# Turning the probabilities in two half-height array tiles, with the short pieces in spare PSUM columns

## The chip, the cores and the metric

The kernel runs on one core of a Trainium2 chip. The metric is the device time of one execution in microseconds (us), taken on that core. Below, PE is TensorE's matmul stream and PEld its weight loads, DVE is VectorE, ACT is ScalarE, POOL is GpSimd and SP is the queue that issues nearly all DMAs.

## The reference

Attention with a bias made from positions, and behind it a two-layer block. What is computed, cut to its core:

```python
scores = (1/sqrt(64)) * q @ k.T                 # 4 batches, 8 heads, 576 positions, 64 wide
x = log1p(|i - j|) / log1p(max(i, 1))           # for each query i and key j
scores += relu(x * w1 + b1) @ w2                # one bias matrix of 576 x 576 for each head
attn = exp(scores - max); attn /= attn.sum(-1) + 1e-9
y = attn @ v                                    # heads side by side: 2304 rows of 512
h = relu(y @ w_in)                              # 512 -> 2048
out = (s * h * h + b) @ w_out                   # 2048 -> 512
```

## The kernel before

It has three stages. Up to about 60 us it builds the bias matrices and writes them to DRAM. Then comes the attention stage, to about 345 us. From there on PE runs the two-layer block nearly without a pause.

The attention stage works on 16 pairs (one head, two batches x = 0 and 1). A pair has five units: units t = 0 to 3 hold 128 query rows of both batches, unit t = 4 holds the last 64 rows of both batches in one 128-row tile. A unit n goes through these operations, in this order:

- `scores(n)`: PE multiplies queries and keys (three float32r products each) into one PSUM tile `sps` of two banks for each x. The 64-row contractions of x = 0 and x = 1 stand in the two halves of the array's rows. The pool `ps_s` has two such tiles, so the next unit's scores need the tiles that this unit's scores left.
- `biased(n, x)` (L242): DVE adds the bias, and takes the row minimum `mn`.
- `expo(n, x)` (L253): ACT takes the exponential into `pr` and sums the row into `su`.
- `probs_t(n, part)`: PE turns `pr` through transposes into PSUM tiles `tps` (pool `ps_t`, two banks), and ACT or DVE copies them to `pt` (512 of the keys) and `ptr` (the last 64 keys of each batch; the "short" transpose).
- `norm(p)` takes the reciprocal of the pair's sums, `norm_t` turns them on PE and copies them to `rt`, `norm_store` and `norm_load` take them through DRAM to `rb`.
- `av(p, kb, hf)`: PE multiplies the values with `pt` or `ptr` into `xps`. At a pair's end DVE multiplies `xps` by `rb` (L340) and a DMA writes the result to `xt` in DRAM.

The order of every engine's queue is the order in which the code is written (a manual schedule). A call `step(n)` with u = n mod 5 issues, for three different units at once, the scores of unit n + 2, the turning of unit n, the exponentials of unit n + 2, and a fifth of the output product of the pair before:

```python
        if ok(m, 0):
            scores(m)
            biased(m, 0)
        if ok(m, 1):
            biased(m, 1)
```

Behind these each step calls `fill()` once or twice (twice for even u). Each call issues one fifth of the decoding of one weight block for the block that follows: first an ACT conversion (L372), then a POOL operation (L374), then three DVE operations (L376, L379, L382). So a pair has eight such calls: in the mean 1.6 conversions on ACT and 4.8 operations on DVE. `split_qk` on POOL (L203, L204) splits the next pair's queries and keys into two float32r parts. At the end of the stage `load_x` and `split_x` (L418) fetch the block's first input from `xt`.

Of the kernel before, what the change touches and what calls it, by code (L numbers as in the profile page):

```python
# [9 lines left out]
F32 = mybir.dt.float32  # L10
# [3 lines left out]
AF = mybir.ActivationFunctionType  # L14
# [12 lines left out]
def attention_moe(ctx, tc, q, k, v, w_in, w_out, dist, par, out):  # L27
    nc = tc.nc
    NB, H, S, D = 2 * q.shape[0], q.shape[1], k.shape[3] - 64, q.shape[2] // 2
# [4 lines left out]
    HALF = S // 2  # L34
# [7 lines left out]
    LAST = 5 * NP  # L42
# [10 lines left out]
    ps_t = ps_ctx.enter_context(tc.tile_pool(name="ps_t", bufs=2, space=PSUM))  # L53
# [13 lines left out]
    ident = const.tile([128, 128], F32, name="ident")  # L67
# [97 lines left out]
    qs, ks, vals, tts, bts, pts, units, accs = {}, {}, {}, {}, {}, {}, {}, {}  # L165
    sums, rows, rts, rbs, bes = {}, {}, {}, {}, {}
# [47 lines left out]
    def scores(n):  # L214
        p, t = divmod(n, 5)
        qt, kt = qs[p], ks[p]
        c = slice(128 * t, 128 * t + 128)
        xs = range(width(n))
        ps = [ps_s.tile([128, 2, 512], F32, tag="s", name="sps") for _ in xs]
        mms = []  # L220
        for hf in range(2):
            for x in xs:
                d = slice(64 * x, 64 * x + 64) if t < 4 else slice(0, 128)
                o = hf * HALF + (64 if x == 0 else 0)
                for i, (a, b) in enumerate(((0, 0), (0, 1), (1, 0))):
                    mms.append((i, hf, x, ps[x][:, hf, 0:HALF], qt[d, a, c], kt[d, b, o:o + HALF]))
        for i, _, _, o, a, b in sorted(mms, key=lambda e: e[1::-1]):
            nc.tensor.matmul(o, a, b, start=(i == 0), stop=(i == 2))  # L228
        units[n] = (
            tp.tile([128, 2, S], F32, tag="pr", name="pr"),  # L230
            sm.tile([128, 2], F32, tag="mn", name="mn"),
            ps,
        )
        if t == 0:
            sums[p] = sm.tile([128, 9], F32, tag="su", name="su")

    def biased(n, x):
# [25 lines left out]
    def norm(p):  # L263
        su = sums.pop(p)
        nc.vector.tensor_scalar(su, su, 1e-9, None, op0=ALU.add)
        nc.vector.reciprocal(su, su)
        rows[p] = su

    def norm_t(p, ps):
        nc.tensor.transpose(ps[0:9, 128:256], rows.pop(p), ident)  # L270
        rt = sm.tile([9, 128], F32, tag="rt", name="rt", bufs=2)
        nc.vector.tensor_copy(rt, ps[0:9, 128:256])
        rts[p] = rt

    def norm_store(p):
# [6 lines left out]
    def norm_load(p):  # L282
        rbs[p] = tp.tile([128, S], F32, tag="rb", name="rb", bufs=2)
        for x in range(2):
            nc.sync.dma_start(out=rbs[p][64 * x:64 * x + 64, :], in_=rs_d[p][x:x + 1, :].broadcast_to([D, S]))

    def probs_t(n, part):
        p, t = divmod(n, 5)
        pr = units[n][0]
        if p not in pts:  # L290
            pts[p] = (ptp.tile([128, 4, 2, S], F32, tag="pt", name="pt"),
                      ptp.tile([128, S], F32, tag="ptr", name="ptr"))
        pt, ptr = pts[p]
        ps = ps_t.tile([128, 512], F32, tag="t", name="tps")
        c = slice(128 * t, 128 * t + 128)
        if t < 4 and part < 2:
            for kb in range(4):
                nc.tensor.transpose(  # L298
                    ps[:, 128 * kb:128 * kb + 128],
                    pr[:, part, 64 * part + 128 * kb:64 * part + 128 * kb + 128], ident)  # L300
            o, i = pt[:, :, part, c], ps.rearrange("p (a b) -> p a b", a=4)
            if part == 0:
                nc.scalar.activation(o, i, AF.Copy)
            else:
                nc.vector.tensor_copy(o, i)
        elif t < 4:
            nc.tensor.transpose(ps[:, 0:128], pr.rearrange("p x j -> p (x j)")[:, 512:640], ident)  # L307
            nc.scalar.activation(ptr[:, c], ps[:, 0:128], AF.Copy)  # L308
        elif part == 0:
            for kb in range(4):  # L310
                nc.tensor.transpose(  # L311
                    ps[:, 128 * kb:128 * kb + 128], pr[:, 0, 128 * kb:128 * kb + 128], ident)
            nc.vector.tensor_copy(
                pt[:, :, :, 512:S], ps.rearrange("p (a x b) -> p a x b", a=4, x=2))
        else:
            nc.tensor.transpose(ps[0:64, 0:128], pr[:, 0, 512:S], ident)  # L316
            for x in range(2):
                nc.scalar.activation(  # L318
                    ptr[64 * x:64 * x + 64, 512:S], ps[0:64, 64 * x:64 * x + 64], AF.Copy)
            norm_t(p, ps)  # L320

    def av(p, kb, hf):
        h, b0 = pairs[p]
        pt, ptr = pts[p]
        vt = vals[p]
        if kb == 0 and hf == 0:
            accs[p] = ps_x.tile([128, 2, 512], F32, tag="x", name="xps")
        ps = accs[p]
        c = slice(hf * HALF, (hf + 1) * HALF)
        if kb < 4:  # L330
            for x in range(2):
                nc.tensor.matmul(ps[64 * x:64 * x + 64, hf, 0:HALF], vt[:, 4 * x + kb, :], pt[:, kb, x, c],  # L332
                                 start=(kb == 0), stop=False)
# [133 lines left out]
    def ok(n, x):  # L467
        return 0 <= n < LAST and x < width(n)
# [7 lines left out]
    def step(n):  # L476
        p, u = divmod(n, 5)
        m = n + 2
        cur = 0 <= n < LAST
        if ok(m, 0):  # L480
            scores(m)
            biased(m, 0)
        if ok(m, 1):
            biased(m, 1)
        if cur and u == 3:
            norm(p)
        if cur:
# [43 lines left out]
    def fill():  # L531
        next(filler, None)
# [16 lines left out]
        26: ((load_bias, 0, 2, 3),),  # L549
        33: ((scores, 0), (biased, 0, 0), (expo, 0, 0), (biased, 0, 1)),  # L550
        35: ((expo, 0, 1), (scores, 1), (biased, 1, 0),
             (expo, 1, 0), (biased, 1, 1), (expo, 1, 1), (load_w, *early[0]), (load_w, *early[1]),
             (load_q, 2), (load_k, 2), (load_v, 1)),
    }
    for st in range(STEPS):
# [74 lines left out]
    for i in range(2, len(todo) + LAG):  # L630
        if i < len(todo):
            c, f = todo[i]
            if c == 0 and f in (6, 10):
# [3 lines left out]
                    name=f"w3{kind}", bufs=1, side=("left", "right")[kind], reuse_waits="tile"))  # L637
# [84 lines left out]
```

## Time and profile before

| | |
|---|---|
| median of 3 runs | 746.71 us (746.08 to 747.33) |
| span of the profiled execution (its own time; the page has no other) | 747.1 us |
| PE busy over the span | 716.6 us (96%) |
| DVE, ACT, POOL busy | 429.3 us (57%), 363.5 us (49%), 186.3 us (25%) |
| attention stage, 180 to 325 us (145 us) | PE busy 140.56 us, DVE 122.98 us, ACT 101.30 us, POOL 45.93 us |

Busy shares of the whole span mix the stages: from 347 us on DVE and ACT have little to do, so what they do in the attention stage has to be read from stretches of that stage alone. A step of the attention stage takes 3.40 us, a pair 16.87 us where nothing is waited for.

### The profile page before, as it was taken

Reading aid. Unit: us, or ns where it says so; the run is one execution under the profiler, and the core shown is the slowest. Engines: PE = TensorE matmul, PEld = TensorE weight load, DVE = VectorE, ACT = ScalarE, POOL = GpSimd, SP = SyncE. Lnnn points to the kernel's source line nnn. Section 1 sums busy time; section 2 is a strip of 40 time slices with the busy share of each in tenths; the row PEclk is TensorE's granted clock in tenths of the full one; section 3 lists DMA queues with packets and bytes.
Section 4 is the critical chain, followed back from the end, with each engine's and each line's share of the span. In section 5 each row is a group of like instructions: output and inputs, shape, how many; then the busy total and the mean of one; then the engine's idle time right before and its main releaser. Section 6 shows DMA issues by size and latency. Waiting matters only on the chain.

```text
span 747.1 us, 12023 instructions
## 1 busy us (share of the span) xinstructions
PE 716.6 (96%) x4530; PEld 534.9 (72%) x4530; DVE 429.3 (57%) x794; ACT 363.5 (49%) x756; POOL 186.3 (25%) x194
## 2 busy tenths in 40 slices
PE   8978999899999999969999999999999999999998
PEld 4436666666666666646888888888888888888896
DVE  7976888788888878963288632233332332223332
ACT  7967767576666667653445322232222332222332
POOL 7991534445333234203654100000000000000000
PEclk9999999999999999989999999999999999999999
DMA  5977765556564765351012130000300002000100
GB/s 171 297 205 245 227 204 170 176 156 212 160 215 134 228 214 184 97 176 60 13 57 85 29 114 0 1 1 0 113 1 0 1 1 84 1 0 1 57 1 28
DMA packets 39817, 76.98 MB, mean 103 GB/s; under 512 B 9040, under 2 KB 12368, under 8 KB 39760
## 3 DMA queue, kind: packets, MB, share of 16 engines
q1 hardware_dynamic: 39616, 75.90, 32.4%
q8 instruction: 35, 0.57, 0.3%
q10 hardware_dynamic: 144, 0.33, 0.1%
q14 instruction: 22, 0.18, 0.1%
HBM read 55.45 MB, written 20.13 MB: 101 GB/s over the span
## 4 chain that ended last, share of the span: by engine, by line
PE 81%; issue 3%; POOL 3%; ACT 2%; DVE 1%; DMA 1%; SPq 1%; DVEq 0%; ACTq 0%; POOLq 0%
PE hps L429 27%; PE o L453 27%; PE sps L228 8%; PE xps L332 7%; PE tps L298 7%; PE xps L335 2%; PE tps L307 2%; PE tps L311 1%; POOL kr L204 1%; ACT ptr L318 1%; DMA x<-xt 1%; POOL qr L204 1%; PE tps L270 1%; POOL full L374 0%; PE tps L316 0%
## 5 line engine op out<-in xcount | busy, mean ns | idle before, releaser
L453 PE MATMUL o<-who,gt 128*128 128x512 f32 x576 | 192.5, 393 | 0.0
L429 PE MATMUL hps<-x,whi 128*128 128x512 f32 (+1 forms) x640 | 184.5, 373 | 0.0
L434 DVE SCALAR_TENSOR_TENSOR r<-r,sb 128x512 f32<-128x512 f32 (+1 forms) x80 | 56.7, 708 | 193.2 <-ACT r L433 193.2
L433 ACT ACTIVATE r<-hps 128x512 f32<-128x512 f32 (+1 forms) x80 | 44.4, 555 | 227.5 <-PE hps L429 227.5
L429 PEld LDWEIGHTS hps<-x,whi 128*128 128x128 f32 x640 | 117.5, 189 | 24.1 <-issue 0.4
L453 PEld LDWEIGHTS o<-who,gt 128*128 128x128 f32 x576 | 108.3, 188 | 24.1
L429 PE MATMUL hps<-x,wli 128*128 128x512 f32 (+1 forms) x320 | 119.0, 372 | 0.0
L253 ACT ACTIVATE pr<-tt,mn 128x576 f32<-128x576 f32 x144 | 110.1, 767 | 10.3 <-DVE mn L242 9.7
L453 PE MATMUL o<-wlo,gt 128*128 128x512 f32 x288 | 113.2, 393 | 0.0
L242 DVE CUSTOM_DVE_ANT_0 tt<-sps,bt 128x576 f32<-128x576 f32 x128 | 91.6, 753 | 29.4 <-PE sps L228 24.0
L228 PEld LDWEIGHTS sps<-kr,qr 64*128 64x128 f32 (+1 forms) x864 | 67.8, 185 | 39.6 <-issue 10.1
L228 PE MATMUL sps<-kr,qr 64*128 64x288 f32 (+1 forms) x864 | 88.3, 311 | 5.8 <-POOL kr L204 2.7
L439 DVE SCALAR_TENSOR_TENSOR gt<-r,sb,gt 128x512 fp32r<-128x512 f32 (+1 forms) x80 | 56.3, 704 | 54.0 <-ACT gt L438 54.0
L438 ACT ACTIVATE gt<-r,sb 128x512 fp32r<-128x512 f32 (+1 forms) x80 | 54.4, 680 | 52.2 <-DVE r L434 52.2
L298 PE MATMUL tps<-ident,pr 128*128 128x128 f32 x512 | 77.1, 282 | 0.3 <-ACT ptr L308 0.3
L332 PE MATMUL xps<-pt,vt 128*64 128x288 f32 x512 | 76.5, 421 | 0.0
L429 PEld LDWEIGHTS hps<-x,wli 128*128 128x128 f32 x320 | 60.3, 188 | 11.1
L298 PEld LDWEIGHTS tps<-ident,pr 128*128 128x128 f32 x512 | 57.7, 142 | 11.4 <-ACT ptr L308 11.2
L453 PEld LDWEIGHTS o<-wlo,gt 128*128 128x128 f32 x288 | 54.2, 188 | 11.6
L374 POOL TENSOR_SCALAR full<-full 128x512 f32<-128x512 f32 x32 | 22.6, 705 | 115.1 <-ACT full L372 114.6
L332 PEld LDWEIGHTS xps<-pt,vt 128*64 128x64 f32 x512 | 31.5, 137 | 24.3 <-issue 10.6
L136 PE MATMUL bps<-f,pt__110 128*32 128x512 f32 x288 | 42.8, 599 | 5.3 <-POOL f L119 2.2
(69 smaller groups left out, 748.1 us busy)
## 6 DMA issues: line engine op xcount, KB each, us to landing
bias<-stg SPq DMA_DIRECT2D x36, 288.0 KB
raw<-in_moe_w_in_dram SPq DMA_DIRECT2D x16, 512.0 KB
raw<-in_moe_w_out_dram SPq DMA_DIRECT2D x16, 512.0 KB
bt<-bias SPq DMA_DIRECT2D x7, 1152.0 KB
qt<-in_q_dram SPq DMA_DIRECT2D x16, 320.0 KB
kt<-in_k_dram SPq DMA_DIRECT2D x16, 320.0 KB
vt<-in_v_dram SPq DMA_DIRECT2D x16, 320.0 KB
rb<-rs SPq DMA_DIRECT2D x32, 144.0 KB
```

Of the source, the lines that this page charges most:

```text
L136: nc.tensor.matmul(pb[32 * c:32 * c + 32, 0:512], w2bd, fs[c][0][:, 0:8], start=True, stop=True)
L228: nc.tensor.matmul(o, a, b, start=(i == 0), stop=(i == 2))
L242: nc.vector.tensor_tensor_reduce(tt.rearrange("p (a b) -> p a b", a=2), ps[x][:, :, 0:HALF], bias.rearrange("p (a b) -> p a b", a=2), -1.0 ...
L253: nc.scalar.activation(pr[:, x], tts.pop((n, x)), AF.Exp, bias=mn[:, x:x + 1], scale=-1.0, accum_out=sums[p][:, col:col + 1])
L298: nc.tensor.transpose(ps[:, 128 * kb:128 * kb + 128], pr[:, part, 64 * part + 128 * kb:64 * part + 128 * kb + 128], ident)
L332: nc.tensor.matmul(ps[64 * x:64 * x + 64, hf, 0:HALF], vt[:, 4 * x + kb, :], pt[:, kb, x, c], start=(kb == 0), stop=False)
L429: nc.tensor.matmul(ps[:, 0:n], w[0, g][:, a, fc], xs_t[c, a][:, j, 0:n], start=(i == 0), stop=(i == 3 * KB - 1))
L433: nc.scalar.activation(r, ps[:, 0:n], AF.Relu)
L434: nc.vector.scalar_tensor_tensor(r, r, sb[:, 0:1], r, op0=ALU.mult, op1=ALU.mult)
L438: nc.scalar.activation(hi, r, AF.Identity, bias=sb[:, 1:2])
L439: nc.vector.scalar_tensor_tensor(lo, r, sb[:, 1:2], hi.bitcast(F32), op0=ALU.add, op1=ALU.subtract)
L453: nc.tensor.matmul(os_t[c][i], gt[:, a, tok], w[1, g][:, fo], start=(f == 0 and j == 0), stop=(f == NF - 1 and j == 2))
```

## The change

The transposes of a unit's probabilities become twice as many of half the size. Rows 0 to 63 and rows 64 to 127 of `pr` are turned separately, in the two halves of the array's rows, alternately, each half into a PSUM bank of its own (the two `ps_t` tiles). The short transpose no longer has a `ps_t` tile: it is written to columns 288 and up of the score tile of the next unit (`spare(n)`), which the scores leave free; the pair's sums go there too. For u = 2 (where the scores that follow use all 128 rows) and for the last two units the transposes keep the full height. The step has a new order: transposes, scores, output product. The exponential of x = 1 leaves the end of its own step and is issued in the next one, behind the copy of the short transpose (`later`).

```diff
+    def spare(n):
+        if n + 1 < LAST - 1:
+            return units[n + 1][2][0][:, :, HALF:]
+        return ps_t.tile([128, 512], F32, tag="t", name="tps").rearrange("p (a b) -> p a b", a=2)
...
+        pss = [ps_t.tile([128, 512], F32, tag="t", name="tps") for _ in range(2)]
+        su = rows.pop(p) if t == 4 else None
+        for i in range(-2, 8):
+            for r in range(2):
+                d = slice(64 * r, 64 * r + 64)
+                if t < 4 and i >= 0:
+                    kb, x = divmod(i, 2)
+                    k0 = 64 * x + 128 * kb
+                    o, b = pss[r][:, 64 * i:64 * i + 64], pr[d, x, k0:k0 + 128]
+                elif t < 4:
+                    if i == -1:
+                        continue
+                    o, b = end[:, r, 0:64], pr[d].rearrange("p x j -> p (x j)")[:, 512:640]
...
+                nc.tensor.transpose(o, b, ident[d, d])
+        if t < 4:
+            nc.scalar.activation(
+                ptr[:, c].rearrange("p (a b) -> p a b", a=2), end[:, :, 0:64], AF.Copy)
...
+        later(n + 1)
+        if t == 4:
+            norm_copy(p, end[0:9, :, 64:128])
...
+            if r == 0:
                 nc.scalar.activation(o, i, AF.Copy)
             else:
                 nc.vector.tensor_copy(o, i)
...
+    def later(n):
+        if (n, 1) in tts:
+            expo(n, 1)
...
+        if cur:
+            probs_t(n)
         if ok(m, 0):
             scores(m)
             biased(m, 0)
...
-        if cur:
-            for part in (2, 0, 1) if u < 4 else (1, 0):
-                probs_t(n, part)
         if ok(m, 0):
             expo(m, 0)
-        if ok(m, 1):
-            expo(m, 1)
         if p >= 1:
             av(p - 1, u, 0)
```

On PE, the steps u = 3 and u = 4 of a pair stood like this before (L228 scores, L307 and L316 short transpose, L298 and L311 the others, L270 the sums, L332 and L335 output product):

```order
L228 MATMUL sps<-kr,qr 128x288 x12
L307 MATMUL tps<-ident,pr 128x128
L298 MATMUL tps<-ident,pr 128x128 x8
L332 MATMUL xps<-pt,vt 64x288 x4
L228 MATMUL sps<-kr,qr 128x288 x12
L316 MATMUL tps<-ident,pr 64x128
L270 MATMUL tps<-ident,su 9x128
L311 MATMUL tps<-ident,pr 128x128 x4
L335 MATMUL xps<-ptr,vt 128x288 x2
```

And now, the same two steps on PE (all half-height transposes are L352):

```order
L352 MATMUL sps<-ident,pr 128x64 x2
L352 MATMUL tps<-ident,pr 128x64 x16
L228 MATMUL sps<-kr,qr 128x288 x12
L387 MATMUL xps<-pt,vt 64x288 x4
L352 MATMUL sps<-ident,pr 64x64 x2
L352 MATMUL sps<-ident,su 9x64 x2
L352 MATMUL tps<-ident,pr 128x64 x8
L228 MATMUL sps<-kr,qr 128x288 x12
L390 MATMUL xps<-ptr,vt 128x288 x2
```

The transposes moved from behind the scores to ahead of them, and the short ones and the sums now write `sps`, the tile of the next unit's scores.

On ACT, the steps u = 3, u = 4 and the start of the next u = 0 stood like this before (L308 and L318 copies of the short transpose, L303 copy to `pt`, L253 exponentials, L372 a conversion of the decoding):

```order
L308 ACTIVATE ptr<-tps 128x128
L303 ACTIVATE pt<-tps 128x4x128
L253 ACTIVATE pr,su<-tt,mn 128x576 x2
L372 ACTIVATE full_986<-raw 128x512
L318 ACTIVATE ptr<-tps 64x64 x2
L253 ACTIVATE pr,su<-tt,mn 128x576 x2
L308 ACTIVATE ptr<-tps 128x128
L303 ACTIVATE pt<-tps 128x4x128
```

And now, the same place on ACT (L354 and L358 copy the short transpose, L369 copies to `pt`, L427 is the conversion):

```order
L354 ACTIVATE ptr<-sps 128x128
L369 ACTIVATE pt<-tps 128x8x64
L253 ACTIVATE pr,su<-tt,mn 128x576
L427 ACTIVATE full_985<-raw 128x512
L358 ACTIVATE ptr<-sps 64x64 x2
L253 ACTIVATE pr,su<-tt,mn 128x576
L369 ACTIVATE pt<-tps 128x4x64
L253 ACTIVATE pr,su<-tt,mn 128x576
L354 ACTIVATE ptr<-sps 128x128
L253 ACTIVATE pr,su<-tt,mn 128x576
```

The two exponentials of a unit have come apart: that of x = 0 stands at the end of its step, ahead of the conversion and of the next copy of a short transpose, and that of x = 1 stands behind that copy.

## Rows read from the trace of the kernel before

**Rows 1.** Stretches: busy us (instructions) per engine, granted clock, DMA share, GB/s.
```profile
79.96:322.41 242.45, 232.07 (x1851) 157.44 (x1849) 204.70 (x458) 165.54 (x416) 90.70 (x86) 0.99 0.57 178
271.76:288.63 16.87, 16.34 (x134) 11.12 (x132) 13.76 (x33) 12.01 (x31) 6.36 (x6) 1.00 0.62 193
```
**Rows 2.** Timeline of PE, one step: start us, us, operation, count.
```profile
189.85 1.07 PE L228 MATMUL sps<-kr,qr 64*128 64x288 f32 x12
190.84 0.33 PE L307 MATMUL tps<-ident,pr 128*128 128x128 f32 x1
191.01 1.19 PE L298 MATMUL tps<-ident,pr 128*128 128x128 f32 x8
192.12 1.19 PE L332 MATMUL xps<-pt,vt 128*64 128x288 f32 x8
193.25 1.06 PE L228 MATMUL sps<-kr,qr 64*128 64x288 f32 x12
```
**Rows 3.** Waits of all engines, 60 to 345 us: total us, times, longest us.
```profile
PEld tps L298 <- ACT ptr L308: 11.2, 63, 0.5
```
**Rows 4.** Timeline of PE in the bias stage.
```profile
30.65 0.47 PE L139 MATMUL bps<-f,pt__110 128*32 128x64 f32 x8
```
**Rows 5.** Timeline of DVE around four steps.
```profile
184.73 0.75 DVE L242 CUSTOM_DVE_ANT_0 tt<-sps,bt 128x576 f32<-128x576 f32 x1
...
192.41 0.17 DVE L265 TENSOR_SCALAR su<-su 128x9 f32<-128x9 f32 x1
192.61 0.22 DVE L266 RECIPROCAL su<-su 128x9 f32<-128x9 f32 x1
192.74 0.63 DVE L305 COPY pt<-tps 128x512 f32<-128x512 f32 x1
...
194.34 0.76 DVE L242 CUSTOM_DVE_ANT_0 tt<-sps,bt 128x576 f32<-128x576 f32 x1 [0.38 <-PE sps L228]
...
195.70 0.27 DVE L272 COPY rt<-tps 9x128 f32<-9x128 f32 x1
...
196.79 0.76 DVE L340 TENSOR_TENSOR rb<-xps,rb 128x576 f32<-128x576 f32 x1 [0.22 <-PE xps L335]
```
**Rows 6.** Timeline of ACT, the same steps.
```profile
185.52 0.78 ACT L253 ACTIVATE pr<-tt,mn 128x576 f32<-128x576 f32 x1
...
186.30 0.76 ACT L253 ACTIVATE pr<-tt,mn 128x576 f32<-128x576 f32 x1
...
191.21 0.28 ACT L308 ACTIVATE ptr<-tps 128x128 f32<-128x128 f32 x1 [1.61 <-PE tps L307]
...
194.57 0.44 ACT L318 ACTIVATE ptr<-tps 64x64 f32<-64x64 f32 x2 [0.82 <-PE tps L316]
```
**Rows 7.** Timeline of PEld, the loads behind the short transpose's copy.
```profile
191.54 0.42 PEld L298 LDWEIGHTS tps<-ident,pr 128*128 128x128 f32 x4 [0.17 <-ACT ptr L308]
```
**Rows 8.** Groups of instructions, 180 to 320 us: busy us, mean ns | idle before.
```profile
L379 DVE SCALAR_TENSOR_TENSOR full<-raw,full 128x512 uint32<-128x512 uint32 x15 | 11.8, 789 | 0.2
L376 DVE TENSOR_SCALAR full<-full 128x512 uint32<-128x512 uint32 x15 | 11.1, 742 | 0.0
...
L372 ACT ACTIVATE full<-raw 128x512 f32<-128x512 f32 x14 | 9.2, 658 | 0.0
```
**Rows 9.** Timeline of PE around the fall of the clock.
```profile
136.76 0.93 PE L228 MATMUL sps<-kr,qr 64*128 64x288 f32 x10 [1.27 <-POOL kr L204]
...
137.87 1.91 PE L298 MATMUL tps<-ident,pr 128*128 128x128 f32 x8
139.71 1.86 PE L332 MATMUL xps<-pt,vt 128*64 128x288 f32 x8
```
**Rows 10.** Stretch behind that wait; columns as in rows 1.
```profile
138.40:141.80 3.40, 3.40 (x19) 2.05 (x19) 2.46 (x8) 2.11 (x5) 0.00 (x0) 0.60 1.04 354
```
**Rows 11.** Timelines of PE and ACT at the end of the attention stage.
```profile
334.38 0.38 PE L270 MATMUL tps<-ident,su 128*9 128x128 f32 x1 [6.02 <-ACT ptr L318]
...
333.36 0.63 ACT L418 ACTIVATE x<-x 128x512 fp32r<-128x512 f32 x1 [1.36 <-DMA x<-xt]
```

More of the change, by code (lines that the diff above doesn't have):

```diff
@@ L267, in norm, with norm_copy @@
         rows[p] = su
-    def norm_t(p, ps):
-        nc.tensor.transpose(ps[0:9, 128:256], rows.pop(p), ident)
+    def norm_copy(p, ps):
         rt = sm.tile([9, 128], F32, tag="rt", name="rt", bufs=2)
-        nc.vector.tensor_copy(rt, ps[0:9, 128:256])
+        nc.vector.tensor_copy(rt if len(ps.shape) == 2 else rt.rearrange("p (a b) -> p a b", a=2), ps)
         rts[p] = rt
@@ L285, in norm_load, with probs_t @@
             nc.sync.dma_start(out=rbs[p][64 * x:64 * x + 64, :], in_=rs_d[p][x:x + 1, :].broadcast_to([D, S]))
-    def probs_t(n, part):
+    def spare(n):
+        if n + 1 < LAST - 1:
+            return units[n + 1][2][0][:, :, HALF:]
+        return ps_t.tile([128, 512], F32, tag="t", name="tps").rearrange("p (a b) -> p a b", a=2)
+    def probs_t(n):
         p, t = divmod(n, 5)
@@ L293, in probs_t @@
         pt, ptr = pts[p]
-        ps = ps_t.tile([128, 512], F32, tag="t", name="tps")
         c = slice(128 * t, 128 * t + 128)
-        if t < 4 and part < 2:
+        end = spare(n)
+        if t < 4 and (t == 2 or n >= LAST - 2):
+            nc.tensor.transpose(end[:, 0, 0:128], pr.rearrange("p x j -> p (x j)")[:, 512:640], ident)
+            nc.scalar.activation(ptr[:, c], end[:, 0, 0:128], AF.Copy)
+            later(n + 1)
+            for x in range(2):
+                ps = ps_t.tile([128, 512], F32, tag="t", name="tps")
+                for kb in range(4):
+                    nc.tensor.transpose(
+                        ps[:, 128 * kb:128 * kb + 128],
+                        pr[:, x, 64 * x + 128 * kb:64 * x + 128 * kb + 128], ident)
+                o, i = pt[:, :, x, c], ps.rearrange("p (a b) -> p a b", a=4)
+                if x == 0:
+                    nc.scalar.activation(o, i, AF.Copy)
+                else:
+                    nc.vector.tensor_copy(o, i)
+            return
@@ L297, in probs_t @@
+        if t == 4 and n >= LAST - 2:
+            nc.tensor.transpose(end[0:64, 0, 0:128], pr[:, 0, 512:S], ident)
+            nc.tensor.transpose(end[0:9, 1, 0:128], rows.pop(p), ident)
+            ps = ps_t.tile([128, 512], F32, tag="t", name="tps")
             for kb in range(4):
                 nc.tensor.transpose(
-                    ps[:, 128 * kb:128 * kb + 128],
-                    pr[:, part, 64 * part + 128 * kb:64 * part + 128 * kb + 128], ident)
-            o, i = pt[:, :, part, c], ps.rearrange("p (a b) -> p a b", a=4)
@@ L302, in probs_t @@
-            if part == 0:
+                    ps[:, 128 * kb:128 * kb + 128], pr[:, 0, 128 * kb:128 * kb + 128], ident)
+            for x in range(2):
+                nc.scalar.activation(
+                    ptr[64 * x:64 * x + 64, 512:S], end[0:64, 0, 64 * x:64 * x + 64], AF.Copy)
+            later(n + 1)
+            norm_copy(p, end[0:9, 1, 0:128])
+            nc.vector.tensor_copy(
+                pt[:, :, :, 512:S], ps.rearrange("p (a x b) -> p a x b", a=4, x=2))
+            return
@@ new lines, in probs_t @@
+        pss = [ps_t.tile([128, 512], F32, tag="t", name="tps") for _ in range(2)]
[11 more added lines that the diff above has]
+                    o, b = end[:, r, 0:64], pr[d].rearrange("p x j -> p (x j)")[:, 512:640]
+                elif i >= 4:
+                    continue
+                elif i >= 0:
+                    o, b = pss[r][:, 64 * i:64 * i + 64], pr[d, 0, 128 * i:128 * i + 128]
+                elif i == -1:
+                    o, b = end[0:9, r, 64:128], su[d]
+                else:
+                    o, b = end[0:64, r, 0:64], pr[d, 0, 512:S]
+                nc.tensor.transpose(o, b, ident[d, d])
@@ new lines, in probs_t @@
+        if t < 4:
+            nc.scalar.activation(
+                ptr[:, c].rearrange("p (a b) -> p a b", a=2), end[:, :, 0:64], AF.Copy)
+        else:
+            for x in range(2):
+                nc.scalar.activation(ptr[64 * x:64 * x + 64, 512:S], end[0:64, x, 0:64], AF.Copy)
+        later(n + 1)
+        if t == 4:
+            norm_copy(p, end[0:9, :, 64:128])
+        for r in range(2):
+            if t < 4:
+                o = pt[:, :, :, 128 * t + 64 * r:128 * t + 64 * r + 64]
+                i = pss[r].rearrange("p (a x b) -> p a x b", a=4, x=2)
+            else:
+                o, i = pt[:, :, r, 512:S], pss[r][:, 0:256].rearrange("p (a b) -> p a b", a=4)
+            if r == 0:
@@ L305, in probs_t @@
                 nc.vector.tensor_copy(o, i)
[L306 to L320, printed above, removed]
+    def later(n):
+        if (n, 1) in tts:
+            expo(n, 1)
     def av(p, kb, hf):
@@ L551, in attention_moe @@
         35: ((expo, 0, 1), (scores, 1), (biased, 1, 0),
-             (expo, 1, 0), (biased, 1, 1), (expo, 1, 1), (load_w, *early[0]), (load_w, *early[1]),
+             (expo, 1, 0), (biased, 1, 1), (load_w, *early[0]), (load_w, *early[1]),
              (load_q, 2), (load_k, 2), (load_v, 1)),
```

## The prediction

> **What bounds the kernel now.** I read the stretches first. In the attention stage PE is busy for 232.07 of 242.45 us, in an undisturbed pair for 16.34 of 16.87 [rows 1]; the reader should see that DVE (13.76) and ACT (12.01) come not far behind. The 242.45 us hold 14 pairs, so a pair takes 17.32 in the mean, 0.45 more than the undisturbed one; most of that is scores that wait for POOL's split of queries and keys, as in [rows 9]. Next comes PE's timeline, for the cost of a step's parts, from the start of one to the start of the next: scores 190.84 - 189.85 = 0.99, transposes 192.12 - 190.84 = 1.28, output product 193.25 - 192.12 = 1.13, together 3.40 [rows 2]. In the transposes, weight loads wait 0.17 for ACT's copy of the short one, 63 times, 11.2 us in all [rows 3, 7]. Behind 345 us nothing changes, so the sum is made for the attention stage, its start and its end.
>
> **What the change removes on PE.** Nine transposes of a step become nine pairs of half ones. The trace has no such pair. Bound below: half of a transpose of today, 1.19 / 8 / 2 = 0.07 [rows 2], if the two halves run side by side. The scores' two 64-row halves do that: six pairs of 288 columns end within 1.06, 0.18 a pair, where eight output products of 288 columns one behind another take 1.19, 0.15 each and so 0.30 for two [rows 2]. Bound above: one half behind the other. Eight matmuls of 64 columns take 0.47 with their tail, 0.06 each at most [rows 4], so 0.12 a pair. I take 0.07, since the scores have the same shape of tile. Transposes then cost 9 x 0.07 + 0.06 for the first load = 0.69 instead of 1.28, and PE's step would be 0.99 + 1.13 + 0.69 = 2.81 (3.26 at the upper bound). The wait for the short copy inside the transposes is gone too. Left alone, this would be worth 0.59 x 60 = 35 us (60 of the 75 steps that have an output product are not u = 2).
>
> **What it adds: a loop through ACT's queue.** The short transpose now lies in a tile that the scores after it must have back. So scores(m) start only when ACT has copied it, and in ACT's queue that copy stands behind the exponential (x = 0) of the scores before. Around that loop, without any decoding:
> - scores start to DVE's first reduction: 194.34 - 193.25 = 1.09 [rows 2, 5]
> - reduction to exponential: 185.52 - 184.73 = 0.79 [rows 5, 6]
> - exponential to the next ACT instruction: 186.30 - 185.52 = 0.78 [rows 6]
> - copy of the short transpose 0.28, and 0.05 until PE loads again (191.54 - 191.49) [rows 6, 7].
>
> Sum 2.99. That is over PE's 2.81, so the loop sets the step, not PE. Before, the same chain had slack: ACT copied the short transpose first and took both exponentials when it liked.
>
> Two kinds of step differ. At u = 2 the transposes stay full: PE needs 0.99 + 1.13 + 1.28 - 0.17 = 3.23. At u = 4 the pair's sums stand in the same tile, and the loop gets longer: 1.09, two reductions 195.70 - 194.34 = 1.36, sum and reciprocal 192.83 - 192.41 = 0.42 [rows 2, 5], turning them 0.33 (as a transpose [rows 2]), two ACT copies 0.44 [rows 6], then DVE's copy to `rt` 0.27 [rows 5], for which the next scores now wait, and two hand-overs of 0.05: 4.0. A pair without decoding: 3 x 2.99 + 3.23 + 4.0 = 16.2, against 16.87.
>
> **What the decoding costs in the new order.** Until now it lay in idle time of ACT and DVE. Now:
> - The ACT conversion, 0.66 [rows 8], stands between the exponential and the short copy, so inside the loop. Per five pairs there are eight. The one at u = 3 hides behind the long loop of u = 4, one hides behind a late reduction, one mostly behind the full transposes. 5 x 0.66 / 5 = 0.65 a pair.
> - DVE has 2.99 + 1.09 - 2.45 = 1.6 from the end of its two reductions to the next, and 0.6 of it for the copy to `pt` (0.63 [rows 5]). A single decoding operation (0.74 or 0.79 [rows 8]) fits into 1.0; two (1.5) make the next reduction late by 0.5, and at u = 4, behind the multiplication by `rb` (0.76 [rows 5]), two make it late by 1.2. Going through the five positions in which the eight calls of a pair can fall, I count 2.2 to 3.3 us late per five pairs, so about 0.55 a pair.
>
> A pair: 16.2 + 0.65 + 0.55 = 17.4. Of the 0.45 of other waits I keep 0.1, since they fall on steps that are late anyway: 17.5, which is 0.18 over today's 17.32. Over the 14.6 pairs of the stage: +2.6 us.
>
> The Trainium skill warns of this case: TensorEngine Tiling (Array Packing), section PSUM Bottleneck, says that tiling speeds up TensorE but not the copying out of PSUM, which may become the bottleneck. The trace has the same columns to copy before and after; the rule gives no time here, and where it didn't hold the sum would be the 35 us of gain above.
>
> **Start, end, clock.** The first pair's five steps have no output product, so PE needs 0.99 + 1.28 = 2.27 there and the loop 2.99: up to 0.7 x 5 = +3.5; part of it lies under DMAs that the first units wait for, I take +1. At the end PE stands still for 6.02, since the sums' transpose waits for ACT's short copy, which stands behind `split_x`, which waits for `x` [rows 11]. In the new order these last transposes and the output product behind them no longer wait, but the first matmul of the block still needs `x`. Its product and the one before, some 3 us of PE's work, move ahead; the last result must go through DRAM as before, and that follows DVE's split: I take -2 (0 to -4).
>
> The granted clock is the last term. After a wait of 1.27 it fell [rows 9]: in 138.40 to 141.80 it was 0.60 in the mean [rows 10], a time at the lower level of 1.2 GHz in it, and eight transposes took 1.91 where 1.19 is usual [rows 2, 9]. Eight output matmuls took 1.86 for 1.19, so one fall costs about 1.4. PE will now be idle for 0.2 to 1.2 in most steps. I take one further fall, +1.2.
>
> Sum: +2.6 + 1 - 2 + 1.2 = +2.8 on the profiled 747.1, so 749.9. The profiled execution is 0.4 over the median of the runs shown (746.71), so I predict **749.5 us**. Copies at u = 4 are shared anew between ACT and DVE (256 columns each instead of 512 on DVE); each hides behind the long loop there. The DMAs are the same in number and size.
>
> **Rivals.**
> 1. *The decoding finds room after all.* If the conversions and the second DVE operations fall where the loop is waiting anyway, a pair stays near 16.2 + 0.4: (16.6 - 17.32) x 14.6 = -10, with start, end and clock 737. For it: ACT is busy for 12.01 of 16.87 only [rows 1]. Against: its idle time lies behind the point where the queue stands. It decides against me once the delays of a pair are under 0.9.
> 2. *The clock keeps falling.* One fall per pair, of which the loop hides a third: 15 x 1.4 x 2/3 = 14, so 762. For it: [rows 9, 10]. Against: waits of about 0.5 at u = 4 in every pair (0.82 on ACT's side [rows 6]) left it at 1.00 in the undisturbed pair [rows 1]. The Trainium skill (TensorE: Matmul & The Clock Gate, Part 4: PE-mode transpose) says that transposes do not count as busy for the clock in the same way; if so, their shortening takes nothing away. The trace has them at full clock, in one stream with other matmuls, and can't tell.
> 3. *The halves don't run side by side.* At 0.12 a pair PE's step is 3.26, over the loop, in the 45 steps of u = 0, 1 and 3: +0.27 each, half of it covered by the delays above: +6, so 755. The step's promise is then not kept at all.
>
> **How the numbers follow.** My forecast gets 0.48; its own range, 744 to 755, takes in the bounds of the end (0 to -4), the start (0 to 3.5) and DVE's delays (0.45 to 0.7). Rival 1 gets 0.27, rival 2 0.15, rival 3 0.10. Measured runs lie within 0.1% of their median, so 0.2% (1.5 us) is about what can be told from no change. Faster: 0.26 of rival 1 and 0.06 of mine, 0.32. Same: 0.15. Slower: 0.28 of mine, 0.15 and 0.10, 0.53. The range 738 to 763 leaves out about half of rival 1's lower end and the far end of rival 2.
>
> **What would show it.** Right: steps of about 3.0 without decoding, 4.0 at u = 4, waits of PE at the scores for ACT's short copy, at u = 4 for DVE's `rt`, and at the short transposes for DVE's reduction; no wait inside the transposes; half pairs at 0.07. Wrong: steps set by PE with 2.8, a clock below 1.00 in many stretches, or scores that wait for nothing while the span is unchanged.

## The result, and the profile after

| | before | after |
|---|---|---|
| median, us | 747.02 (4 runs, 746.08 to 747.41) | 754.43 (4 runs, 754.14 to 756.22) |
| span of the profiled execution, us | 747.1 | 754.4 |
| mean granted clock over the span | 0.993 | 0.988 |

The changed kernel is slower: ratio 1.0095, 95% interval 1.0078 to 1.0112. That is +7.4 us by the medians and +7.3 by the spans, where +2.8 was forecast.

To place the 7.3 I cut both timelines of PE at the same work: the first output product of a u = 0 (that of the first pair), and the one 14 pairs later. The first fence has these rows of before, the second those of after.

```profile
75.44 0.95 PE L332 MATMUL xps<-pt,vt 128*64 128x288 f32 x6
...
317.89 1.19 PE L332 MATMUL xps<-pt,vt 128*64 128x288 f32 x8
```

```profile
79.24 1.23 PE L387 MATMUL xps<-pt,vt 128*64 128x288 f32 x4
...
325.66 1.19 PE L387 MATMUL xps<-pt,vt 128*64 128x288 f32 x8
```

- start: 79.24 - 75.44 = +3.8
- 14 pairs: 246.42 (325.66 - 79.24) against 242.45, +4.0, or 17.60 a pair against 17.32
- end: 754.4 - 325.66 = 428.7 against 747.1 - 317.89 = 429.2, -0.5

Next the stretches of after, with the columns of [rows 1]: the 14 pairs, an undisturbed pair, the start, and two places further on.

```profile
79.24:325.66 246.42, 215.68 (x2312) 147.89 (x2311) 197.06 (x455) 163.95 (x430) 91.59 (x88) 0.99 0.56 174
268.63:284.79 16.16, 15.05 (x165) 10.46 (x165) 13.10 (x33) 11.34 (x31) 5.21 (x5) 1.00 0.68 197
64.00:84.00 20.00, 15.27 (x145) 11.73 (x145) 11.02 (x29) 11.56 (x32) 2.16 (x3) 0.74 0.95 312
302.00:307.00 5.00, 4.74 (x39) 3.55 (x41) 3.50 (x9) 3.17 (x9) 0.00 (x0) 0.66 0.35 120
357.00:362.00 5.00, 4.30 (x12) 3.43 (x13) 3.07 (x3) 0.72 (x1) 1.77 (x2) 0.66 0.08 21
```

PE is now idle for 30.7 us of the 14 pairs, where [rows 1] has 10.4: PE has less to do and waits for more. The clock is low at the start (0.74 over 20 us), at 302 and at 357. Before, it was low at two places, that of [rows 10] and one around the wait of 6.02 in [rows 11], where the prediction does not mention the clock; this is the stretch of before around it:

```profile
325.00:347.00 22.00, 15.98 (x81) 10.52 (x77) 7.30 (x13) 5.44 (x12) 0.00 (x0) 0.84 0.51 170
```

The clean steps of after in PE's timeline:

```profile
269.62 1.24 PE L390 MATMUL xps<-ptr,vt 128*128 128x288 f32 x4
...
272.53 1.19 PE L387 MATMUL xps<-pt,vt 128*64 128x288 f32 x8
273.65 0.28 PE L352 MATMUL sps<-ident,pr 64*128 64x64 f32 x2
273.76 0.66 PE L352 MATMUL tps<-ident,pr 64*128 64x64 f32 x16
274.24 1.33 PE L228 MATMUL sps<-kr,qr 64*128 64x288 f32 x12
275.50 1.19 PE L387 MATMUL xps<-pt,vt 128*64 128x288 f32 x8
...
276.96 1.04 PE L307 MATMUL tps<-ident,pr 128*128 128x128 f32 x8
277.75 1.04 PE L228 MATMUL sps<-kr,qr 128*128 128x288 f32 x6
...
281.80 1.19 PE L387 MATMUL xps<-pt,vt 128*64 128x288 f32 x8
282.92 0.25 PE L352 MATMUL sps<-ident,pr 64*64 64x64 f32 x2
283.71 0.23 PE L352 MATMUL sps<-ident,su 64*9 64x64 f32 x2 [0.55 <-DVE su L266]
283.77 0.41 PE L352 MATMUL tps<-ident,pr 64*128 64x64 f32 x8
284.00 0.37 PE L228 MATMUL sps<-kr,qr 64*128 64x288 f32 x1
284.79 1.06 PE L228 MATMUL sps<-kr,qr 64*128 64x288 f32 x11 [0.42 <-DVE rt L271]
285.78 1.24 PE L390 MATMUL xps<-ptr,vt 128*128 128x288 f32 x4
...
287.54 0.37 PE L228 MATMUL sps<-kr,qr 64*128 64x288 f32 x1
288.28 0.93 PE L228 MATMUL sps<-kr,qr 64*128 64x288 f32 x10 [0.37 <-ACT ptr L354]
```

All transposes of a step now take 274.24 - 273.65 = 0.59, the 16 half ones among them that go to `tps` 0.48, so 0.06 a pair. The eight full ones at u = 2, which wait for nothing, take 277.75 - 276.96 = 0.79, 0.10 each. A pair of halves has as many columns to write as one full transpose and takes 0.06 us for it: the halves do run side by side. From one output product to the next it is 2.91 (272.53 - 269.62) or 2.97 (275.50 - 272.53), and 3.98 at u = 4 (285.78 - 281.80), where PE waits for the sums and then for `rt`.

ACT around the same steps shows the loop:

```profile
273.43 0.78 ACT L253 ACTIVATE pr<-tt,mn 128x576 f32<-128x576 f32 x1 [0.69 <-DVE mn L242]
274.11 0.19 ACT L253 ACTIVATION_READ_ACCUMULATOR pr<-tt,mn 128x1 f32 x1
274.20 0.26 ACT L354 ACTIVATE ptr<-sps 128x128 f32<-128x128 f32 x1
...
287.40 0.67 ACT L427 ACTIVATE full<-raw 128x512 f32<-128x512 f32 x1
287.98 0.25 ACT L354 ACTIVATE ptr<-sps 128x128 f32<-128x128 f32 x1
```

The copy of the short transpose starts when the exponential is through, at 274.20, though its transpose was written 0.3 before; with a conversion (287.40) between them it starts 0.58 later still, and the scores at 288.28 wait for it. The waits of all engines, 60 to 345 us (total, times, longest):

```profile
PE sps L352 <- DVE su L266: 10.0, 15, 0.9
PE sps L228 <- ACT ptr L354: 8.3, 17, 0.6
PE sps L352 <- DVE mn L242: 7.1, 12, 1.0
PE sps L228 <- DVE rt L271: 6.5, 15, 0.5
PE sps L301 <- DVE mn L242: 3.5, 4, 1.3
...
PE sps L228 <- POOL kr L204: 0.8, 2, 0.6
```

The wait inside the transposes [rows 3] is gone. The first five stand in its place (L301 is the short transpose of full height at u = 2); for POOL's split PE now waits for 0.8 only.

### The profile page after: what moved, and what is told of

Read it like the earlier page. It is cut to its first block, busy times and chain, and to the rows that moved or that the text cites. A ratio compares the mean times of both kernels' runs of the same rounds, so it can differ in the third digit from the quotient of the medians.

```text
span 754.4 us, 13111 instructions
## 1 busy us (share of the span) xinstructions
PE 700.8 (93%) x5043; PEld 527.1 (70%) x5043; DVE 422.7 (56%) x794; ACT 360.4 (48%) x771; POOL 184.2 (24%) x194
## 4 chain that ended last, share of the span: by engine, by line
PE 70%; DVE 10%; ACT 6%; DMA 6%; issue 5%; POOL 1%; SPq 0%; DVEq 0%; ACTq 0%; POOLq 0%
PE o L508 27%; PE hps L484 25%; PE sps L228 8%; DVE tt L242 4%; PE xps L387 3%; ACT pr L253 3%; PE bps L136 2%; DMA bias<-stg 2%; PE tps L307 1%; ACT full L427 1%; PE tps L352 1%; DMA raw<-in_moe_w_in_dram 1%; DVE full L434 1%; DMA rs<-rt 1%; PE sps L352 1%
## 5 line engine op out<-in xcount | busy, mean ns | idle before, releaser
L253 ACT ACTIVATE pr<-tt,mn 128x576 f32<-128x576 f32 x144 | 111.3, 773 | 87.7 <-DVE mn L242 87.2
L228 PE MATMUL sps<-kr,qr 64*128 64x288 f32 (+1 forms) x864 | 107.4, 319 | 16.5 <-ACT ptr L354 8.3
L228 PEld LDWEIGHTS sps<-kr,qr 64*128 64x128 f32 (+1 forms) x864 | 79.6, 190 | 27.8 <-ACT ptr L354 14.9
L119 POOL TENSOR_SCALAR f<-ls,thr 128x576 f32<-128x576 f32 x60 | 43.2, 751 | 4.4 <-DVE ls L97 4.2
L117 DVE TENSOR_SCALAR f<-ls,thr 128x576 f32<-128x576 f32 x60 | 43.4, 795 | 0.0
```

Source lines behind the costliest of these rows:

```text
L117: nc.vector.tensor_scalar(f, src, thr[:, col], None, op0=ALU.max)
L253: nc.scalar.activation(pr[:, x], tts.pop((n, x)), AF.Exp, bias=mn[:, x:x + 1], scale=-1.0, accum_out=sums[p][:, col:col + 1])
```

## The experiments

In the table, "clean" is the shortest of 14 times from one output product to the next, for the u of the later one, and "pair" the mean over the 14 pairs, clock falls and all other waits in it. Ratios are against the kernel before on the same chip. Its median there was 747.0 beside after, 748.0 beside e1, e2, e3 and e5, 748.9 beside e6 to e9 and 747.9 beside the others, so a difference between two medians of the table can be off by some 2 us.

| kernel | median, us | ratio (95%) | clean u = 0, 1, 2, 3, 4 | clean sum | pair |
|---|---|---|---|---|---|
| before | 747.0 | | 3.33 3.39 3.25 3.39 3.50 | 16.86 | 17.32 |
| after | 754.4 | 1.0095 (1.0078 to 1.0112) | 2.91 2.96 3.04 3.07 3.98 | 15.96 | 17.60 |
| e1_old_order | 799.5 | 1.067 (1.0627 to 1.0713) | 3.78 3.84 4.27 3.83 3.51 | 19.23 | 20.42 |
| e5_old_order_full | 807.6 | 1.0804 (1.0757 to 1.0851) | 4.22 4.27 4.26 4.26 3.52 | 20.53 | 21.35 |
| e2_conv_behind | 752.0 | 1.0058 (1.0031 to 1.0084) | 2.90 2.96 3.04 3.07 3.97 | 15.94 | 17.30 |
| e3_full_height | 763.0 | 1.0195 (1.0173 to 1.0218) | 3.13 3.24 3.04 3.24 3.97 | 16.62 | 17.96 |
| e6_expo_behind | 747.8 | 0.9985 (0.9961 to 1.0008) | 2.80 2.76 3.04 2.75 4.00 | 15.35 | 17.13 |
| e7_sums_apart | 740.2 | 0.9884 (0.9838 to 0.9929) | 3.10 2.96 3.04 3.08 2.47 | 14.65 | 16.76 |
| e8_both | 732.9 | 0.9796 (0.9761 to 0.9831) | 2.80 2.76 3.04 2.75 2.56 | 13.91 | 16.23 |
| e9_both_full | 738.5 | 0.9872 (0.9804 to 0.994) | 3.13 3.24 3.04 3.24 2.58 | 15.23 | 16.65 |
| d1_no_dve_decode | 748.0 | 0.9996 (0.9973 to 1.0019) | 2.91 2.96 3.05 3.07 3.98 | 15.97 | 17.21 |
| d2_no_conversion | 752.2 | 1.0076 (1.0042 to 1.0109) | 2.91 2.97 3.04 3.07 3.97 | 15.96 | 17.22 |
| e10_early_store | 721.7 | 0.9648 (0.9615 to 0.9681) | 2.80 2.76 3.04 2.75 2.57 | 13.92 | 16.07 |

My theory: the loop through ACT's queue and the sums at u = 4 set the step, and the decoding lengthens both. Rivals: DVE's queue bounds it whatever the order is; or the halves are what counts.

### The halves in the old order: e1_old_order, e5_old_order_full

```diff
     def spare(n):
-        if n + 1 < LAST - 1:
-            return units[n + 1][2][0][:, :, HALF:]
+        if n + 2 < LAST:
+            return units[n + 2][2][0][:, :, HALF:]
...
     def later(n):
-        if (n, 1) in tts:
-            expo(n, 1)
+        pass
...
-        if cur:
-            probs_t(n)
         if ok(m, 0):
             scores(m)
             biased(m, 0)
         if ok(m, 1):
             biased(m, 1)
         if cur and u == 3:
             norm(p)
+        if cur:
+            probs_t(n)
         if ok(m, 0):
             expo(m, 0)
+        if ok(m, 1):
+            expo(m, 1)
```

e5 is e1 with `t == 2` in `probs_t` widened to all t < 4 (full height). Expected of e1:

> The changed kernel with the order of before (scores, transposes, both exponentials, output product); the half transposes stay, and the short ones and the sums go to the spare columns of the score tile just written, so the next scores, which need that tile, come a whole output product later. Theory 'the loop through ACT's queue sets the step': without the loop PE's 0.99 + 0.59 + 1.13 = 2.71 sets it, or DVE with its 13.1 to 13.8 per pair; a pair of 14.2 to 15.2, total 700 to 720. Rival 'DVE or the decoding bounds it whatever the order': a pair stays at 16.5 to 17.5, total 738 to 752.

And of e5:

> As e1_old_order, with full-height transposes for every unit of 128 rows: of the change only the spare columns are left, so the wait for the short copy inside the transposes is gone. Theory 'PE sets the step of the old order': 0.99 + 0.93 + 1.13 = 3.05 instead of 3.40, a pair of 15.2 to 15.8, total 717 to 730; against e1 the halves are then worth 0.34 x 45 = 15 at most, less where DVE takes over. Rival 'the wait was covered': within 3 us of the kernel before, 744 to 750.

Both were far slower than either theory said: 799.5 and 807.6. PE's and DVE's timelines of e1 (PE first) show why:

```profile
204.47 1.06 PE L228 MATMUL sps<-kr,qr 64*128 64x288 f32 x12
206.72 0.27 PE L352 MATMUL sps<-ident,pr 64*128 64x64 f32 x2 [1.19 <-DVE mn L242]
206.83 0.66 PE L352 MATMUL tps<-ident,pr 64*128 64x64 f32 x16
207.42 1.19 PE L386 MATMUL xps<-pt,vt 128*64 128x288 f32 x8
```

```profile
205.91 0.74 DVE L242 CUSTOM_DVE_ANT_0 tt<-sps,bt 128x576 f32<-128x576 f32 x1
```

The short transpose into the spare columns of the tile just written starts when DVE's reduction of that tile's other columns ends (205.91 + 0.74 = 206.65). The spare columns are free as columns, not in time. So putting them into the newer tile didn't open the loop; it made a longer one: scores, reduction, transposes, output product, 3.8 to 4.3. My expectation had left this wait out. The same wait stands in the kernel after (7.1 us in the list above), where it is short, since the tile there is a unit older. e5 against e1 is the halves' price with the transposes in that loop: 8 us by the medians. By the pairs of the table it is 0.93 a pair, 13 us in 14 pairs; e1 gave part of it back at the start, where its clock was lower (first output product at 84.15, e5's at 78.61).

### The loop through ACT's queue: e6_expo_behind

```diff
     def later(n):
-        if (n, 1) in tts:
-            expo(n, 1)
+        for x in range(2):
+            if (n, x) in tts:
+                expo(n, x)
...
-        if ok(m, 0):
-            expo(m, 0)
```

> The changed kernel, with both exponentials of a unit issued behind the next copy of a short transpose (before, that of x = 0 stood ahead of it). Theory 'the exponential ahead of the short copy closes the loop': at u = 0, 1 and 3 the step falls from 2.91 to 3.05 to PE's 2.71 or so, and the conversion's 0.57 no longer shows; u = 4 keeps its 3.98. About 1.1 a pair, 16 us: 735 to 743. Rival 'DVE's queue sets the step anyway': within 3 us of the changed kernel, 751 to 756.

In the clean steps this is what came: 2.76, 2.75 and 2.80 where after has 2.96, 3.07 and 2.91; u = 4 stayed at 4.00. PE's timeline:

```profile
236.36 1.19 PE L388 MATMUL xps<-pt,vt 128*64 128x288 f32 x8
237.49 0.28 PE L352 MATMUL sps<-ident,pr 64*128 64x64 f32 x2
237.59 0.67 PE L352 MATMUL tps<-ident,pr 64*128 64x64 f32 x16
238.13 1.07 PE L228 MATMUL sps<-kr,qr 64*128 64x288 f32 x12
239.13 1.19 PE L388 MATMUL xps<-pt,vt 128*64 128x288 f32 x8
```

239.13 - 236.36 = 2.77, PE without a wait. The whole gained 6.6 us against after (754.4 to 747.8) and not the 11 to 19 expected: late steps stayed late. The mean step at u = 1 is 3.47 where after has 3.50, at u = 2 it is 3.42 where after has 3.23, and PE's wait at the short transposes for DVE's reduction (`mn`) rose from 7.1 to 12.8 us. It is no faster than before.

### The sums at u = 4, and both: e7_sums_apart, e8_both, e9_both_full

This is e7's edit, against after; e8 has e6's besides, and e9 also the full height of e3 below.

```diff
                 elif i == -1:
-                    o, b = end[0:9, r, 64:128], su[d]
+                    o, b = pss[r][0:9, 320:384], su[d]
                 else:
-                    o, b = end[0:64, r, 0:64], pr[d, 0, 512:S]
+                    o, b = pss[r][0:64, 256:320], pr[d, 0, 512:S]
...
         if cur:
             probs_t(n)
+        if cur and u == 3:
+            norm(p)
         if ok(m, 0):
             scores(m)
             biased(m, 0)
         if ok(m, 1):
             biased(m, 1)
-        if cur and u == 3:
-            norm(p)
```

> The changed kernel, with the pair's sums taken ahead of the next two reductions on DVE, and with the short transposes and the sums of u = 4 in unused columns of the ps_t tiles instead of the score tile; the exponentials stay where the change put them. Theory 'u = 4 loses 1 us a pair to the sums': the step at u = 4 falls from 3.98 to about 3.0, 15 us in all: 737 to 744. Rival 'the next step gives it back, since DVE is late there': 750 to 755.

> e6 and e7 together. If both loops are what the change cost: about 31 us less than the changed kernel, 718 to 730, a pair of 15.2. If DVE, busy for 13.1 to 13.8 of a pair, takes over: 732 to 742.

> e8 with full-height transposes for every unit of 128 rows, which prices the halves once no loop hides them. If PE sets e8's step: 0.34 more at u = 0, 1 and 3, 13 to 15 us over e8. If DVE sets it: under 5 us over e8.

e7 measured 740.2, in the theory's range: the clean step at u = 4 fell from 3.98 to 2.47, and 0.2 came back at u = 0. This was the largest single cost. e7 moves two things at once, the place of the sums in DVE's queue and their place in PSUM; after waits for both (10.0 us for `su`, 6.5 for `rt`), and no run tells the two apart. e8 measured 732.9, 21.5 under after. That is not in the range of the theory of the two loops (718 to 730) but at the fast end of the one in which DVE takes over (732 to 742): its clean pair is 13.91, but its mean pair 16.23. DVE is busy for 196.8 of the 227.3 us of the 14 pairs, 14.06 a pair, so the mean pair could not be under that; what makes up the other 2.2 no run takes apart. e9 prices the halves: +5.6 (738.5, its runs spread from 734.2 to 745.2), near the 5 of the DVE side, though its clean steps at u = 0, 1 and 3 are 0.33 to 0.49 longer. So most of what the halves save on PE does not reach the time; that it falls into waits for DVE is my reading.

In e8 a new wait shows. DVE's and PE's timelines, and the stretch around them:

```profile
268.82 0.76 DVE L400 TENSOR_TENSOR rb<-xps,rb 128x576 f32<-128x576 f32 x1 [4.31 <-DMA rb<-rs]
```

```profile
269.63 2.19 PE L392 MATMUL xps<-pt,vt 128*64 128x288 f32 x8 [3.31 <-DVE rb L400]
```

```profile
268.00:275.00 7.00, 4.74 (x38) 3.22 (x38) 5.19 (x9) 2.14 (x6) 2.40 (x3) 0.56 0.94 294
```

The pair's sums come back from DRAM too late for the faster pair, PE waits for 3.31, and the clock falls behind it (0.56).

### The price of full height: e3_full_height

```diff
-        if t < 4 and (t == 2 or n >= LAST - 2):
+        if t < 4:
```

> The changed kernel with full-height transposes for every unit of 128 rows; the new order and the spare columns stay. Theory 'the loop sets the step': PE's step becomes 0.99 + 0.93 + 1.13 = 3.05, just over the loop's 2.9 to 3.0, and the decoding's delays cover part of it: +1 to +5, 755 to 760. Rival 'PE sets the step, the halves are worth their 0.34 each time': 0.34 x 45 = +15, 769.

It measured 763.0, 8.6 over after: between the two ranges. The clean steps are at PE's 3.13 to 3.24 (0.99 + 0.93 + 1.13 = 3.05 and some hand-over), 0.17 to 0.28 over the loop. So the loop hid somewhat under half of the 15 that the halves save on PE, not nearly all of it.

### The decoding: e2_conv_behind, d1_no_dve_decode, d2_no_conversion

e2 moves the conversion, and the POOL operation that needs it, behind the copies of the next step's transposes:

```diff
-        nc.scalar.activation(full, raw[:, :, 1].bitcast(F32), AF.Abs)
+        held.append(lambda: nc.scalar.activation(full, raw[:, :, 1].bitcast(F32), AF.Abs))
...
         if cur:
             probs_t(n)
+        release()
```

> The changed kernel, with the decoding's conversion on ACT issued behind the copies of the transposes of the next step, and no longer between the exponential and the short copy. Theory 'conversions lie in the loop': each saves 0.57 us at the steps u = 0, 1 and partly 4, about 0.6 a pair, so 744 to 748. Rival 'they only move the wait elsewhere (the next exponential comes later by as much)': within 1.5 us of the changed kernel's 754.4.

d1 and d2 leave parts of the stage's decoding out:

```diff
         nc.scalar.activation(full, raw[:, :, 1].bitcast(F32), AF.Abs)
         yield
-        nc.gpsimd.tensor_scalar(full, full, highest, lowest, op0=ALU.min, op1=ALU.max)
+        if g == 3:
+            nc.gpsimd.tensor_scalar(full, full, highest, lowest, op0=ALU.min, op1=ALU.max)
```

(d1; the three DVE operations likewise. The blocks with g == 3 are decoded only behind this stage.)

```diff
-        nc.scalar.activation(full, raw[:, :, 1].bitcast(F32), AF.Abs)
+        src_ = full
+        if g == 3:
+            nc.scalar.activation(full, raw[:, :, 1].bitcast(F32), AF.Abs)
+        else:
+            src_ = raw[:, :, 1].bitcast(F32)
         yield
-        nc.gpsimd.tensor_scalar(full, full, highest, lowest, op0=ALU.min, op1=ALU.max)
+        nc.gpsimd.tensor_scalar(full, src_, highest, lowest, op0=ALU.min, op1=ALU.max)
```

(d2.)

> The changed kernel without the POOL and DVE operations of the decoding in the attention stage (the ACT conversions stay; the weights that it would have decoded are left raw, so the block computes with other numbers). By the forecast's sum DVE's share of the decoding costs 0.55 a pair, 8 us over 14.6 pairs: 745 to 748. Rival 'DVE's decoding delays nearly every late step, the 4.2 to 4.5 at u = 0 among them': 0.9 to 1.2 a pair, 736 to 742.

> The changed kernel without the decoding's conversions on ACT in the attention stage (POOL reads the raw words instead, so the block computes with other numbers; POOL's and DVE's operations stay). By the forecast's sum the conversions cost 0.65 a pair, 9.5 us: 743 to 747. Rival 'they cost what moving them saved, about 2 to 4 us': 750 to 753.

e2 measured 752.0, in neither of its ranges, d1 748.0, at the end of the theory's, and d2 752.2, in the rival's. d1 took 6.4 us from after, 0.44 a pair over 14.6 pairs, where the forecast had 0.55. Without the conversions it was 2.3 us (d2), and 2.4 for moving them (e2): 0.16 a pair, where the forecast had 0.65. By the pairs of the table, one execution each, it is 0.39 for d1, 0.38 for d2 and 0.30 for e2. So the conversions cost 0.16 to 0.38 a pair, well under the forecast either way. In the steps themselves the conversion does cost what was said: the 3.47 to 3.49 that after shows at u = 0 in six of 14 pairs is 2.93 or less in all pairs of e2 and d2. But other steps got longer at the same time: u = 1 of e2 (3.67 in the mean, 3.50 in after), u = 4 of d2 (4.41, and 4.17), and the step that waits longest for POOL's split (u = 3 of the fourth pair: 5.02 in e2 and 5.19 in d2, 3.94 in after). So the delays partly cover one another, and a sum that adds them counts that part twice; no run leaves both parts of the decoding out, so the size of that overlap is not shown.

### The best version: e10_early_store

Against e8:

```diff
         if cur and u == 3:
             norm(p)
+        if cur and u == 4:
+            norm_store(p)
         if ok(m, 0):
...
-            if u == 4:
-                norm_store(p)
...
-    for work in (att, xsp, xsp, xsp, xsp, att, h0, att, h0, att,
+    for work in (att, att, xsp, xsp, xsp, xsp, h0, att, h0, att,
```

> e8 with the pair's sums stored to DRAM ahead of the output's DMA in SP's queue (in e8 the store stands behind that DMA, which waits for the multiplication by rb, which waits for the sums of the pair before), and at the end of the stage the sums and the short copies ahead of the split of x on DVE and ACT. Theory 'the sums' round trip through DRAM is the next loop': e8's waits of PE for rb (5.9 us, one of 3.3) and the fall of the clock behind them go, and 2 to 3 us at the end: 720 to 728. Rival 'the round trip is late because the DMA engines are busy, not because of the queue': 730 to 735.

It measured 721.7, ratio 0.9648 against before (0.9615 to 0.9681): the theory's range. PE's wait for `rb` in the stage, first in e8 and then in e10 (60 to 345 us):

```profile
PE xps L392 <- DVE rb L400: 5.9, 5, 3.3
PE xps L392 <- DVE rb L400: 0.5, 1, 0.5
```

The end of the stage is 722.5 - 299.81 = 422.7 from the same output product on, 6.0 shorter than in after. Why, its DVE shows, and that of after behind it:

```profile
311.35 0.28 DVE L275 COPY rt<-tps 9x128 f32<-9x128 f32 x1 [0.92 <-ACT ptr L328]
...
325.68 0.75 DVE L400 TENSOR_TENSOR rb<-xps,rb 128x576 f32<-128x576 f32 x1
```

```profile
340.53 1.36 DVE L474 TENSOR_TENSOR x<-x 128x512 fp32r<-128x512 f32 x2 [0.29 <-ACT x L473]
341.80 0.27 DVE L271 COPY rt<-tps 9x128 f32<-9x128 f32 x1
...
356.80 0.76 DVE L395 TENSOR_TENSOR rb<-xps,rb 128x576 f32<-128x576 f32 x1 [4.10 <-DMA rb<-rs]
```

PE at that place of after:

```profile
357.70 0.49 PE L508 MATMUL o<-who,gt 128*128 128x512 f32 x1 [3.10 <-DVE rb L395]
```

In after the last `rt` stands behind the split of `x`, and its trip through DRAM keeps the last pair, and PE with it (3.10 at 357.70), waiting; in e10 this last `rb` is multiplied without a wait. The clean pair is e8's, so what e10 adds is this end (422.7, e8 427.7) and the earlier store (a mean pair of 16.07, e8 16.23); one run holds both, and only the place in the trace tells them apart.

## Why the prediction was right, and where its sum was off

The sign and the range held (+7.4 against +2.8; 738 to 763), and the mechanism is shown, not only argued: the loop by e6, the sums by e7 (its two moves together), both by e8. That the sum came so near is in part luck, since terms missed in both directions. Term by term:

1. *Half transposes* (0.69 for a step's, 0.07 a pair): 0.59 and 0.06. Right; rival 3 is out, and e9 shows the halves at work where no loop hides them. The way there was less sound. The 1.19 of the bound below has the wait of 0.17 in it; by the 0.10 of a full transpose that waits for nothing, half is 0.05. The output products with which the scores are compared do not run one behind another: eight of 64 columns of the array take 1.19, and four of 128 take 1.24, so they too go two at a time. What shows the scores' halves side by side is u = 2, where six products of 128 rows take 1.04 and twelve of 64 rows 1.06. The eight matmuls of [rows 4] go to four groups of 32 partitions, so their 0.06 is no price of one behind the other either. And the 35 us count the steps u = 4, which turn six pieces and not nine, like the others.
2. *The loop* (2.99; 3.23 at u = 2; 4.0 at u = 4; a clean pair of 16.2): 2.91 to 3.07, 3.04, 3.98, together 15.96, and 16.16 in a pair that has some decoding. Right.
3. *Decoding* (0.65 for ACT, 0.55 for DVE): 0.16 to 0.38, and 0.39 to 0.44, by what leaving it out saves. The ACT term was mis-sized: it was added to delays that it partly covers. That the waits for it exist was right.
4. *Other waits* (0.1 of the 0.45): from the clean 15.96 to the mean 17.60 it is 1.64, of which the decoding's two prices explain 0.6 to 0.8. Of the rest, 0.8 to 1.0, some is PE's waits at the short transposes for late reductions (7.1 and 3.5 us from 60 to 345) and some the falls of the clock; it is not split further, and it is not POOL, for whose split PE waits 0.8 us in all. So the pair came out at 17.60 against 17.5 because one term was too large and another too small.
5. *Start* (+1, 3.5 at most): +3.8. This is the term that failed most. The five steps without an output product leave PE idle, as was said, but the granted clock was then 0.74 over 64 to 84 us. In e8, without the loops, that stretch shows 1.00 and the first output product starts at 74.50 (74.82 in e10), 4.7 before that of after:

```profile
64.00:84.00 20.00, 16.81 (x206) 12.81 (x206) 15.94 (x41) 16.07 (x43) 5.33 (x5) 1.00 0.94 305
```

   Over the kernels the start goes with that clock: 75.44 at 1.00 in before, 77.34 at 0.91 in e9, 80.03 at 0.74 in e6, 84.15 at 0.57 in e1. e9 has neither loop, so their absence alone does not keep the clock up, and how much of the 3.8 is the loop and how much the clock stays open. The fall was forecast once, as a term of its own (+1.2); at the start it hit a stretch that was already priced without it.
6. *End* (-2): -0.5. The last transposes moved ahead of the wait for `x`, as was said, but the last `rt` did not, and the clock fell again behind the wait for it (0.66 at 357 to 362), as it had in the end of before (0.84 over 325 to 347). e10 shows that the whole end was worth 6 us, that fall included.
7. *Rivals.* The decoding did not find room (rival 1). The clock did not fall once in every pair (rival 2), but at the start, at 302 and at 357. DVE, which the prediction names as close behind PE, is the next bound by what e8 shows (busy for 14.06 of a mean pair of 16.23); it is not what bound the kernel after.

The prediction took the span for the execution's own time. The profiled run of after took 756.22 with a span of 754.4, so 1.8 lie around a span. The forecast stays the same without that step, since 746.71 + 2.8 is 749.5 too. Its spread of 0.1% was too narrow: later runs of the kernel before went from 745.4 to 750.8.

The rule from the Trainium skill (TensorEngine Tiling (Array Packing), section PSUM Bottleneck), that faster TensorE may leave the copying out of PSUM as the bottleneck, turned out to name the right place: the queue that copies the short transposes set the step at 2.9 to 3.1, where PE needs 2.75 (e6). The trace adds that here it is not the copying's amount, but its place in ACT's queue.

## What to carry to other kernels

Before a scratch result goes into unused columns of a tile that is in rotation, follow who must release that tile: the copy that empties the columns joins the loop between one use of the tile and the next, with all that stands ahead of it in its engine's queue. A faster engine's saving counts only down to the length of the longest such loop. To shorten the loop, put the releasing copy first in its queue, and take what a whole step waits for (here the sums) off the rotating tile. Where two delays can fall on the same step, price them by leaving them out, one at a time and together, and not by adding them.

## What the runs showed of the hardware

- A transpose into columns of a PSUM tile that DVE was not reading started only when DVE's reduction of the tile's other columns had ended (206.72 after 206.65 in e1, 1.19 waited). In the same way DVE's `rt` waits in after for ACT's copy out of the same tile (7.6 us in 14 waits, 0.8 at most), which is part of u = 4's 3.98. The Trainium skill (PSUM — Partial Sum Buffer, section PSUM bank collisions raise a hardware error) says that no two engines may access one bank in the same partitions at a time, at other columns either, and that the program must keep them apart; these waits, which are for the program's semaphores, agree. I had read that rule as one on data, and priced e1 without it.
- Of one kernel, the time goes with the mean granted clock of the run: the six runs of e10 took 718.3 to 719.1 us at 0.995 to 0.997 and 724.3 to 725.3 at 0.983 to 0.992. The Trainium skill (TensorE: Matmul & The Clock Gate, section HAM oscillation — how this bites in real kernels) tells of a clock that falls again when TensorE waits between bursts of work; the traces agree in that the falls looked at here stand behind waits of PE (3.31 with 0.56 behind it in e8), while the 0.55 and 0.42 at u = 4 left it at 1.00 in the pair shown. So a few us between two kernels can be a fall more or less.
